# R of the lists built for 32 tokens at once, v tiles loaded behind the tokens, and a new timetable for splits, fills and checks in a Fourier-mixing plus expert-lookup kernel

## The chip, the cores and the metric

One core of one Trainium2 chip. The metric is the device time in microseconds of one execution. The kernel before has a median of 1169.77 us over 3 runs (1169.46 to 1169.96).

## The reference

```python
def _A_ref(x, dft_seq_re, dft_seq_im, dft_hid_re, dft_hid_im):   # x: 2048 x 512
    a = jnp.einsum("bsd,ed->bse", x, dft_hid_re)
    b = jnp.einsum("bsd,ed->bse", x, dft_hid_im)
    return jnp.einsum("ts,bse->bte", dft_seq_re, a) - jnp.einsum("ts,bse->bte", dft_seq_im, b)

def _B_ref(x, w_q, k1, k2, u, v):          # 32 heads, 64 + 64 keys of 128, 4096 experts of 512
    q = jnp.einsum("nd,dhc->nhc", xf, w_q)
    s1 = jnp.einsum("nhd,ed->nhe", q[..., :dk], k1)
    s2 = jnp.einsum("nhd,ed->nhe", q[..., dk:], k2)
    # the two largest of s1 and of s2, their four sums, the two largest of these: top_s, top_e
    g = _softmax(top_s, axis=-1)
    act = _gelu(jnp.einsum("nd,nhkd->nhk", xf, u[top_e]))
    return jnp.einsum("nhk,nhk,nhkd->nd", g, act, v[top_e])

xn = _layernorm(x, axis=-1)
return x + _A_ref(xn, ...) + _B_ref(xn, ...)
```

## The kernel before, in words

**Start (0 to about 85 us).** The tokens are normalised, the Fourier part runs as matmuls on folded matrices, and the tokens are transposed and split into two float16 parts (`xq`, also stored to `xt_d`).

**Score part (about 85 to 459 us).** Eight stages `j` of four heads, each with 16 blocks `i` of 128 tokens; 16j + i is the number by which tables place work. For a block PE does 12 matmuls (`scores`, L801) into one of four PSUM banks; ACT evicts the bank into a score tile `ss` (L806, four buffers); DVE takes the largest values and their indices (L809, L813). Beside that run, placed by tables of block numbers (`todo`, `at_k`, `slots`):

- `m_prep`: the raw weights `wq` of the next stage are split into two float16 parts, `wh` on ACT (L162), then a scaling of the raw tile on ACT (L167) or POOL (L169), then a subtraction on POOL (L170). Four tiles t a stage; PE multiplies them with the keys at L148 in blocks 3, 4, 5 and 7.
- `fill_uv`: the expert tables u and v are loaded, scaled twice on ACT (L613, L614) and split on POOL (L615) into resident tiles. `fill_far` does the same for v tiles 11 to 15, in blocks 104, 105, 106, 110 and 111, and stores them to DRAM (`v_d`), since their place in SBUF is taken until the score part ends.
- checks of the symmetries of the Fourier matrices (`compare`): two loads, a difference on POOL (L758, L764), and on the next block two absolute sums on ACT (L784 over 896 columns, L785 over 128). `EARLY` names the 32 that are done here; 36 others are done in the expert part.
- `routing` of the stage before, in blocks 1, 2 and 4: three sums on POOL (L651 to L653), comparisons on DVE (L654 onward), an exp on ACT (L659), casts into `z`.

Before a long ACT instruction of a fill, split or scale, `behind` copies the scale (128x1, L570) into spare columns of that block's score tile, and the instruction reads its scale from there.

**Passage.** The routing tile `z` goes to DRAM (`z_d`, L907); the first two blocks' lists are turned and widened (`cmp`, L704 and L705).

**Expert part (459 us to the end).** 15 blocks of 128 tokens (the 16th is done by gathers, one token's row at a time, on the side). For a block PE multiplies tokens `xb` with all u tiles (`u_part`, L959), ACT applies gelu (L962), and the gates come from `g_mm`: per half of 32 tokens (16) DVE compares the lists with counters into L (16 x 128 columns, L985) and R (16 x 32 columns, L990, then times the gate, L993), and PE multiplies L by R (L995). Products (L1005, L1012, L1015) feed `v_part` (L1024) over v tiles 0 to 15. Three pairs of L and R rotate. The other checks, and sums over weights (`fit`), run beside it in even steps.

Each engine works its queue in order; a planner fixes the order from the program's order and from hints that set order alone (`follow`, `hold`). SP issues nearly all loads and stores in order.

Of the kernel before, what the change touches and what calls it, by code (L numbers as in the profile page):

```python
# [36 lines left out]
def tile_fnet_peer(ctx, tc, x, ca, cb, c5, wt, wf, wr, wq, kt, ut, vn, uv, out):  # L37
# [55 lines left out]
    EARLY = [*range(8, 24), *range(40, 56)]  # L93
    early = cst.tile([P, 2, len(EARLY)], F32, name="early")
# [19 lines left out]
    k_sb = cst.tile([P, 2, 64], F32, name="k_sb")  # L114
    nc.sync.dma_start(k_sb, kt)
# [24 lines left out]
    def m_mul(j, t, kds):  # L140
        for kd in kds:
            if t == 0:
                MS.setdefault((j, "p"), []).append((pc if kd < 2 else pb)(f"m{j}_{kd}"))
            for hh in range(2):
                c0 = (t * 2 + hh) * 64
                if (j, t, "h") in MS:
                    for n, (l, r) in enumerate(((0, 0), (0, 1), (1, 0))):
                        nc.tensor.matmul(MS[j, "p"][kd][:, c0:c0 + 64],  # L148
                                         MS[j, t, "l" if l else "h"][:, hh, kd * P:(kd + 1) * P],
                                         k16[:, r, t // 2, :], start=n == 0, stop=n == 2)  # L150
                    continue
                nc.tensor.matmul(MS[j, "p"][kd][:, c0:c0 + 64], MS[j, t][:, hh, kd * P:(kd + 1) * P],
                                 k_sb[:, t // 2, :], start=True, stop=True)

    def m_prep(j, t, pool, at):

        raw = MS[j, t].rearrange("p h k -> p (h k)")
        MS[j, t, "h"] = pool.tile([P, 2, D], F16, tag="wh", name=f"wh{j}_{t}", bufs=4)
        h = MS[j, t, "h"].rearrange("p h k -> p (h k)")
        l = raw.bitcast(F16)[:, 0:2 * D]  # L160
        MS[j, t, "l"] = l.rearrange("p (h k) -> p h k", h=2)
        nc.scalar.activation(h, raw, AF.Copy, scale=at)  # L162
        if j == 1 and t % 2:
            nc.vector.scalar_tensor_tensor(l, raw, sw, h, op0=ALU.mult, op1=ALU.subtract)
            return
        if j == 1 or t > 1:
            nc.scalar.activation(raw, raw, AF.Copy, scale=at)  # L167
        else:
            nc.gpsimd.tensor_scalar(raw, raw, sw, None, op0=ALU.mult)  # L169
        nc.gpsimd.tensor_tensor(l, raw, h, op=ALU.subtract)  # L170
# [20 lines left out]
    def m_scale(j, pm, at=None):  # L191
# [10 lines left out]
        if w == 3:  # L202
            nc.scalar.activation(m[:, 0, 0:2].rearrange("p k n -> p (k n)"),
                                 MS[j, 3].rearrange("p h k -> p (h k)"), AF.Abs, accum_out=mx[:, KD + 1:KD + 2])
            nc.scalar.activation(m[:, 0, 0, 0:P], k_sb.rearrange("p w k -> p (w k)"), AF.Abs,
                                 accum_out=mx[:, KD + 2:])
# [27 lines left out]
    xtp = stS.enter_context(tc.tile_pool(name="xtp", bufs=1, side="left"))  # L234
    xq = [xtp.tile([P, 4, 2, KD, P], F16, name=f"xq{g}") for g in range(4)]
# [259 lines left out]
    nc.scalar.activation(k16[:, 0], k_sb, AF.Copy, scale=sk)  # L495
    nc.vector.scalar_tensor_tensor(k16[:, 1], k_sb, sk, k16[:, 0], op0=ALU.mult, op1=ALU.subtract)
# [58 lines left out]
    def part_b(safe, stS, stP, stE, xt, u_sb, cmp_p):  # L555
# [10 lines left out]
        def behind(src, at):  # L566

            if at is None:
                return src
            nc.scalar.activation(at, src, AF.Copy)  # L570
            return at


# [6 lines left out]
        def absmax(which, g, at):  # L580
            nc.scalar.activation(uf[15], uf[15], AF.Abs, scale=behind(one, at), accum_out=asums[:, g, which:which + 1])
# [22 lines left out]
        def fill_uv(which, g, at=None, dst=None):  # L604
            if dst is None:
                dst = (u_sb if which == 0 else v_sb)[g]
            s = behind(su if which == 0 else sv, at)
# [16 lines left out]
        def fill_far(g, at):  # L624
            t = wq_tile(f"vs{g}").rearrange("p h k -> p (h k)").bitcast(F16)
# [87 lines left out]
        def hold(f, after):  # L713
# [3 lines left out]
            for i in made[first:]:  # L717
                if i.engine in (mybir.EngineType.DVE, mybir.EngineType.Activation, mybir.EngineType.Pool):
# [7 lines left out]
        def compare(n, at=None):  # L726
# [54 lines left out]
            def judge():  # L781
                k = n if at is None else at
                a, b = (chk, asum) if at is None else (early[:, 0], early[:, 1])
                nc.scalar.activation(tf[:, P:], tf[:, P:], AF.Abs, accum_out=a[:, k:k + 1])  # L784
                nc.scalar.activation(tf[:, :P], tf[:, :P], AF.Abs, accum_out=b[:, k:k + 1])  # L785
# [9 lines left out]
        def scores(j, i, vals, idx):  # L795
# [8 lines left out]
            st = sp.tile([P, 520], F32, tag="s", name=f"ss{j}_{i}", bufs=3 if safe else 4)  # L804
            s = st[:, 0:512].rearrange("p (g e) -> p g e", g=2 * HC)
            nc.scalar.activation(s.rearrange("p g e -> p (g e)"), ps, AF.Copy, scale=inv)  # L806
# [9 lines left out]
            return st[:, 512:], mm  # L816
# [13 lines left out]
        else:  # L830
# [18 lines left out]
        for g, n in zip(range(V2, 16), () if safe else (104, 105, 106, 110, 111)):  # L849
# [8 lines left out]
        at_k = [13, 15] + [16 * j + i for j in range(1, 6) for i in (7, 8, 9, 10)]  # L858
        at_k += [101, 103, 108, 112, 118, 120, 122, 124, 125, 126]
# [7 lines left out]
        for j in range(NCH):  # L867
# [8 lines left out]
            for i in range(NT):  # L876
# [25 lines left out]
                for n, f in enumerate(todo[j * NT + i]):  # L902
                    f(spare[:, n:n + 1])
# [11 lines left out]
        LR = [(lr.tile([P, 16, P], F16, name=f"L{k}"), lr.tile([P, 16, NC], F16, name=f"R{k}")) for k in range(3)]  # L915
# [14 lines left out]
        for g in range(V2, 16 if not safe else V2):  # L930
            nc.sync.dma_start(v_sb[g].rearrange("p l c d -> p (l c d)"), v_d[g - V2])
# [7 lines left out]
        def prep(b):  # L939
            xb, act = BT[b] if b < 2 else blk_tiles(b)  # L940
            if b:
                nc.sync.dma_start(xb.rearrange("p a k n -> p (a k n)"), xt_d[b])
# [31 lines left out]
        def g_mm(b, tg, after=None):  # L974
            cmp = CMP[b]
            p = pg(f"g{b}_{tg}")
            for hf in range(2):
                ts = slice(tg * TG + hf * 16, tg * TG + hf * 16 + 16)

                def bc(w, n):  # L980
                    return cmp[:, w, ts, :].unsqueeze(2).to_broadcast([P, 16, n // 2, 2])

                LR.append(LR.pop(0))
                L, R = LR[-1]
# [3 lines left out]
                    bc(0, P), op=ALU.is_equal)  # L988
                Rv = R.rearrange("p t (c two) -> p t c two", two=2)
                nc.vector.tensor_tensor(  # L990
                    Rv, io_c.rearrange("p (c two) -> p c two", two=2).unsqueeze(1).to_broadcast([P, 16, NC // 2, 2]),
                    bc(1, NC), op=ALU.is_equal)
                nc.vector.tensor_tensor(Rv, Rv, bc(2, NC), op=ALU.mult)  # L993
                for t in range(16):
                    i = nc.tensor.matmul(p[:, hf, t * NC:(t + 1) * NC], L[:, t, :], R[:, t, :], start=True, stop=True)  # L995
# [226 lines left out]
        if not safe:  # L1222
            nc.vector.memset(chk[:, 68:70], 0.0)
            for k in range(0, len(EARLY), 16):
                for w, c in enumerate((chk, asum)):
                    nc.vector.tensor_copy(c[:, EARLY[k]:EARLY[k] + 16], early[:, w, k:k + 16])
        prep(0)
        prep(1)
        stP.close()
# [87 lines left out]
    with tc.If(r2 > 0):  # L1317
# [8 lines left out]
        xtp = stS.enter_context(tc.tile_pool(name="xtp2", bufs=1, side="left"))  # L1326
        xt = [xtp.tile([P, 2, KD, P], F16, name=f"xs{i}") for i in range(NT)]
# [127 lines left out]
```

## Time and profile before

| | |
|---|---|
| median of 3 runs | 1169.77 us |
| the profiled execution | 1169.36 us |
| its span in the trace | 1167.5 us |
| mean granted TensorE clock | 0.986 |
| score part, first to last block on PE | about 72 to 459 us |
| expert part, one block on PE | 45.5 us |

Rows of the stretches read: from:to, length, then busy us and instructions (x) of PE, weight loads, DVE, ACT and POOL, then the granted clock, the DMA share and GB/s. Rows of the waits read: who <- whom: us in total, times, longest. Timeline rows read: start, length, engine, line, operation, count, and in brackets the idle time before it with what ended it. Group rows read: count | busy us, mean ns | idle before, with what ended it.

### The profile page before, as it was taken

Reading aid. Unit: us, or ns where it says so; the run is one execution under the profiler, and the core shown is the slowest. Engines: PE = TensorE matmul, PEld = TensorE weight load, DVE = VectorE, ACT = ScalarE, POOL = GpSimd, SP = SyncE. Lnnn points to the kernel's source line nnn. Section 1 sums busy time; section 2 is a strip of 40 time slices with the busy share of each in tenths; the row PEclk is TensorE's granted clock in tenths of the full one; section 3 lists DMA queues with packets and bytes.
Section 4 is the critical chain, followed back from the end, with each engine's and each line's share of the span. In section 5 each row is a group of like instructions: output and inputs, shape, how many; then the busy total and the mean of one; then the engine's idle time right before and its main releaser. Section 6 shows DMA issues by size and latency. Waiting matters only on the chain.

```text
span 1167.5 us, 29293 instructions
## 1 busy us (share of the span) xinstructions
PE 1115.2 (96%) x11681; PEld 732.7 (63%) x11681; DVE 906.0 (78%) x2790; ACT 670.3 (57%) x1257; POOL 480.0 (41%) x442
## 2 busy tenths in 40 slices
PE   5799999999999988699999999999999999999997
PEld 4354555454444434696786786876876867868763
DVE  7878888797977978767888777677878876777861
ACT  3575666877867877332654654654646455556450
POOL 0021848678778777100413433334233243233320
PEclk9899999999999999899999999999999999999999
DMA  8255254442533463622445535443554355355401
GB/s 311 78 214 202 84 188 163 127 161 76 180 130 106 152 201 97 216 69 73 119 132 164 166 98 171 148 140 112 163 168 130 115 163 164 116 153 157 110 11 48
DMA packets 75074, 162.79 MB, mean 139 GB/s; under 512 B 9254, under 2 KB 26157, under 8 KB 74928
## 3 DMA queue, kind: packets, MB, share of 16 engines
q1 hardware_dynamic: 63250, 123.07, 31.8%
q0 software_dynamic: 11520, 37.75, 11.8%
q8 instruction: 93, 1.52, 0.5%
q14 instruction: 53, 0.43, 0.1%
q10 hardware_dynamic: 158, 0.01, 0.0%
HBM read 143.96 MB, written 16.84 MB: 138 GB/s over the span
## 4 chain that ended last, share of the span: by engine, by line
PE 74%; POOL 11%; DVE 6%; issue 4%; DMA 2%; ACT 1%; SPq 0%; POOLq 0%; DVEq 0%; ACTq 0%
PE v L1024 27%; PE z L959 26%; PE s L801 13%; PE g L995 4%; POOL cx L758 2%; POOL v L615 2%; PE p L370 2%; POOL u L615 2%; POOL wq L169 1%; POOL wq L170 1%; PE m L148 1%; POOL vs L615 1%; DVE vals L809 1%; DMA xb<-xt_d 1%; DVE idx L813 1%
## 5 line engine op out<-in xcount | busy, mean ns | idle before, releaser
L801 PE MATMUL s<-m,xq 128*128 128x512 f16 x1536 | 341.7, 380 | 10.1 <-ACT ss L806 10.0
L959 PE MATMUL z<-xb,u 128*128 128x128 f16 x5760 | 333.4, 220 | 12.3 <-DMA xb<-xt_d 8.4
L959 PEld LDWEIGHTS <-u 128*128 128x128 f16 x5760 | 326.8, 98 | 16.0 <-issue 13.0
L1024 PE MATMUL v<-v,act 128*128 128x512 f16 x1440 | 319.9, 379 | 0.0
L801 PEld LDWEIGHTS <-xq 128*128 128x128 f16 x1536 | 148.8, 98 | 184.1 <-issue 14.8
L1084 POOL TENSOR_TENSOR ov<-ov,ga 128x512 f32<-128x512 f32 x64 | 95.0, 1484 | 396.7 <-ACT ga L1079 319.7
L1024 PEld LDWEIGHTS <-act 128*128 128x128 f16 x1440 | 137.5, 98 | 156.7
L985 DVE TENSOR_TENSOR L<-io_lam,cmp 128x2048 f16<-128x2048 f16 x120 | 150.3, 1253 | 102.3 <-PE g L995 71.4
L962 ACT ACTIVATE act<-z,scl 128x512 f32<-128x512 f32 x120 | 81.6, 682 | 192.0 <-PE z L959 188.3
L809 DVE MAX8 vals<-ss 128x8 f32<-128x64 f32 x1024 | 152.9, 216 | 21.9 <-ACT ss L806 21.8
L1050 POOL DMA_INDIRECT ga<-in_uv_dram,eix x64 | 93.4, 1460 | 52.1 <-PE z L959 24.5
L1015 DVE TENSOR_TENSOR act<-w,act 128x1024 f16<-128x1024 f32 x60 | 80.1, 1336 | 41.5 <-ACT act L1012 38.4
L813 DVE FIND_INDEX8 idx<-vals,ss 128x8 uint16<-128x256 f32 x256 | 107.2, 419 | 0.0
L1012 ACT ACTIVATE act<-w 128x1024 f16<-128x1024 f32 x60 | 80.8, 1346 | 21.1 <-DVE w L1005 21.0
L806 ACT ACTIVATE ss<-s,wsc 128x512 f32<-128x512 f32 x112 | 74.3, 675 | 24.2 <-PE s L801 22.3
L784 ACT ACTIVATE cx<-cx 128x896 f32<-128x896 f32 x64 | 60.6, 947 | 31.2 <-POOL cx L764 11.3
L1005 DVE SCALAR_TENSOR_TENSOR w<-act,scl,g 128x1024 f32<-128x1024 f32 x60 | 76.0, 1273 | 1.4 <-ACT fit L1152 1.1
L758 POOL TENSOR_TENSOR cx<-cx 128x512 f32<-128x512 f32 (+2 forms) x56 | 61.7, 1120 | 20.4 <-DMA cx<-in_cb_dram 18.2
L170 POOL TENSOR_TENSOR wq<-wq,wh 128x1024 f16<-128x1024 f32 x26 | 55.4, 2132 | 19.7 <-DMA wq<-in_wq_dram 16.1
L995 PEld LDWEIGHTS <-L 128*128 128x128 f16 x1920 | 55.8, 96 | 8.5 <-issue 1.8
L995 PE MATMUL g<-R,L 128*128 128x32 f16 x1920 | 57.5, 176 | 1.4 <-DVE R L993 1.4
L993 DVE TENSOR_TENSOR R<-R,cmp 128x512 f16<-128x512 f16 x120 | 57.1, 476 | 2.0
(276 smaller groups left out, 1255.7 us busy)
## 6 DMA issues: line engine op xcount, KB each, us to landing
cx<-in_cb_dram SPq DMA_DIRECT2D x64, 448.0 KB
wq<-in_wq_dram SPq DMA_DIRECT2D x32, 512.0 KB
fit<-in_wq_dram SPq DMA_DIRECT2D x28, 512.0 KB
uv<-in_ut_dram SPq DMA_DIRECT2D x16, 512.0 KB
uv<-in_vn_dram SPq DMA_DIRECT2D x16, 512.0 KB
xq<-in_x_dram SPq DMA_DIRECT2D x8, 512.0 KB
xt_d<-xq SPq DMA_DIRECT2D x16, 256.0 KB
cx<-in_ca_dram SPq DMA_DIRECT2D x64, 64.0 KB
```

Of the source, the lines that this page charges most:

```text
L758: v_eng.tensor_tensor(v, v, tv[:, 0:1].to_broadcast([P, len(ix), 256]), op=o)
L801: mm = nc.tensor.matmul(ps, xt[i][:, l, kd, :], m[:, r, kd, :], start=(n == 0), stop=(n == 3 * KD - 1))
L809: nc.vector.max(vals[:, i, w, :, h], s[:, g, :])
L813: nc.vector.max_index(idx[:, i, w].rearrange("p k h -> p (k h)"), vals[:, i, w, 0:2].rearrange("p k h -> p (k h)"), s[:, w * HC:g + 1, :]. ...
L959: mm = nc.tensor.matmul(p[:, cc * P:(cc + 1) * P], ug[:, l, c % 2, kd, :], xb[:, r, kd, :], start=(n == 0), stop=(n == 3 * KD - 1))
L962: GL[mm.ins.name] = nc.scalar.activation(act[:, cg * 4:cg * 4 + 4, :].rearrange("p c n -> p (c n)"), p, AF.Gelu_apprx_tanh, scale=zsc)
L985: nc.vector.tensor_tensor(L.rearrange("p t (l two) -> p t l two", two=2), io_lam.rearrange("p (l two) -> p l two", two=2).unsqueeze(1).to_ ...
L995: i = nc.tensor.matmul(p[:, hf, t * NC:(t + 1) * NC], L[:, t, :], R[:, t, :], start=True, stop=True)
L1012: i = nc.scalar.activation(w16[..., 0], w, AF.Copy)
L1024: mm = nc.tensor.matmul(pv, w16[:, c, :, l], vg[:, r, c % 2, :], start=(c == 0 and k == 0), stop=(c == NC - 1 and k == 2))
L1050: nc.gpsimd.indirect_dma_start(out=t, out_offset=None, in_=uv, in_offset=bass.IndirectOffsetOnAxis(ap=eix[:, n].rearrange("p k h -> p (k h ...
L1084: T["a"] = nc.gpsimd.tensor_tensor(o, o, t, op=ALU.add)
```

## The change

- `g_mm`: R is built once for 32 tokens (32 x 32 columns) with its first half and used by both; two R buffers in place of three; L stays at 16 tokens and three buffers.
- The loads of v tiles 11 to 15 stand behind the load of block 1's tokens (`xb`) in SP's queue.
- `behind` and its copies go. The ACT work of a block is kept behind that block's eviction by an order hint (`hold` with ACT alone).
- `m_prep`: of the later stages, only tile 0 is scaled on POOL; tile 1 is scaled on ACT as 2 and 3 are. The four tiles come one block earlier (11, 13, 15 of the stage before, and 1).
- Fills of stages 3 to 6 move from blocks 4, 6, 11, 13 to 3, 5, 12, 14; the far fills from 104 to 111 to block 10 of stages 2 to 6, through a buffer of the checks (`cx`).
- 28 checks in place of 32 in the score part, in blocks 0, 4, 6 and 7 of most stages; four move to the expert part. An early check sums 896 columns only; its other sum is set to zero.
- The key tile `k_sb` moves to the pool of the tokens; the score tile loses its 8 spare columns.

```diff
-    EARLY = [*range(8, 24), *range(40, 56)]
-    early = cst.tile([P, 2, len(EARLY)], F32, name="early")
+    EARLY = [*range(8, 24), *range(40, 52)]
+    early = cst.tile([P, len(EARLY)], F32, name="early")
...
-        if j == 1 or t > 1:
+        if j == 1 or t:
             nc.scalar.activation(raw, raw, AF.Copy, scale=at)
         else:
             nc.gpsimd.tensor_scalar(raw, raw, sw, None, op0=ALU.mult)
...
-        def behind(src, at):
-            if at is None:
-                return src
-            nc.scalar.activation(at, src, AF.Copy)
-            return at
...
         def fill_far(g, at):
-            t = wq_tile(f"vs{g}").rearrange("p h k -> p (h k)").bitcast(F16)
+            t = sp.tile([P, 4, 4, 64], F32, tag="cx", name=f"vs{g}", bufs=3)
+            t = t.rearrange("p s q c -> p (s q c)").bitcast(F16)
...
             def judge():
                 k = n if at is None else at
-                a, b = (chk, asum) if at is None else (early[:, 0], early[:, 1])
+                a = chk if at is None else early
                 nc.scalar.activation(tf[:, P:], tf[:, P:], AF.Abs, accum_out=a[:, k:k + 1])
-                nc.scalar.activation(tf[:, :P], tf[:, :P], AF.Abs, accum_out=b[:, k:k + 1])
+                if at is None:
+                    nc.scalar.activation(tf[:, :P], tf[:, :P], AF.Abs, accum_out=asum[:, k:k + 1])
...
-                    todo[1 + t if j == 1 else (j - 1) * NT + 2 * t - 4].append(
-                        lambda at, j=j, t=t: m_prep(j, t, wqp, behind(sw, at)))
+                    todo[1 + t if j == 1 else (j - 1) * NT + 2 * t - 5].append(
+                        lambda at, j=j, t=t: m_prep(j, t, wqp, sw))
...
-        slots = [29, 31, 36, 43, 45] + [16 * j + i for j in range(3, 7) for i in (4, 6, 11, 13)]
+        slots = [29, 31, 36, 43, 45] + [16 * j + i for j in range(3, 7) for i in (3, 5, 12, 14)]
...
-        for g, n in zip(range(V2, 16), () if safe else (104, 105, 106, 110, 111)):
+        for g, n in zip(range(V2, 16), () if safe else [16 * j + 10 for j in range(2, 7)]):
...
-        at_k = [13, 15] + [16 * j + i for j in range(1, 6) for i in (7, 8, 9, 10)]
-        at_k += [101, 103, 108, 112, 118, 120, 122, 124, 125, 126]
+        at_k = [10, *(16 + i for i in (0, 4, 6, 7, 10)), *(16 * j + i for j in range(2, 7) for i in (0, 4, 6, 7)), 112, 125]
...
-                for n, f in enumerate(todo[j * NT + i]):
-                    f(spare[:, n:n + 1])
+                for f in todo[j * NT + i]:
...
+                        hold(lambda: f(None), spare, (mybir.EngineType.Activation,))
...
-        for g in range(V2, 16 if not safe else V2):
-            nc.sync.dma_start(v_sb[g].rearrange("p l c d -> p (l c d)"), v_d[g - V2])
...
         prep(0)
         prep(1)
+        for g in range(V2, 16 if not safe else V2):
+            i = nc.sync.dma_start(v_sb[g].rearrange("p l c d -> p (l c d)"), v_d[g - V2])
+            follow(i.ins, T["xb"])
...
             for hf in range(2):
-                LR.append(LR.pop(0))
-                L, R = LR[-1]
+                LS.append(LS.pop(0))
+                L = LS[-1]
...
+                if hf == 0:
+                    RS.append(RS.pop(0))
+                    R = RS[-1]
+                    Rv = R.rearrange("p t (c two) -> p t c two", two=2)
+                    nc.vector.tensor_tensor(
+                        Rv, io_c.rearrange("p (c two) -> p c two", two=2).unsqueeze(1)
+                        .to_broadcast([P, TG, NC // 2, 2]), bc(1, 0, TG, NC), op=ALU.is_equal)
+                    nc.vector.tensor_tensor(Rv, Rv, bc(2, 0, TG, NC), op=ALU.mult)
```

SP's queue at the passage, before: `z_d` is the store of the routing, `v_d` the far v tiles, `xb` the tokens of block 1, `oy` and `zb` loads for later blocks.

```order
L907 DMA z_d<-z 128x12x384
L931 DMA v_5929<-v_d 128x2048
L931 DMA v_5930<-v_d 128x2048
L931 DMA v_5931<-v_d 128x2048
L931 DMA v_5932<-v_d 128x2048
L931 DMA v_5933<-v_d 128x2048
L942 DMA xb_5940<-xt_d 128x1024
```

The same place in SP's queue after the change:

```order
L905 DMA z_d<-z 128x12x384
L939 DMA xb_5812<-xt_d 128x1024
L1230 DMA v_5806<-v_d 128x2048
L1230 DMA v_5807<-v_d 128x2048
L1230 DMA v_5808<-v_d 128x2048
L1230 DMA v_5809<-v_d 128x2048
L1230 DMA v_5810<-v_d 128x2048
```

The tokens' load has moved from behind the five v tiles to ahead of them. Next, ACT's queue at the boundary from stage 4 to stage 5, before: `ss` are evictions (from `s`) and, from `wsc`, the small copies; `wh` and `wq` are splits, `m` a sum over weights, `c` the exp of the routing.

```order
L806 ACTIVATE ss_15_3961<-s_15_3948,wsc 128x512
L570 ACTIVATE ss_0_3988<-wsc 128x1
L189 ACTIVATE m_4382,sums<-m_3744 128x2048
L162 ACTIVATE wh_2_4001<-wq_2_3792,ss_0_3988 128x1024
L806 ACTIVATE ss_0_3988<-s_0_3975,wsc 128x512
L167 ACTIVATE wq_2_3792<-wq_2_3792,ss_0_3988 128x1024
L659 ACTIVATE c_0_4032<-c_0_4030 128x64
L806 ACTIVATE ss_1_4018<-s_1_4005,wsc 128x512
```

The same boundary in ACT's queue after the change (`cx` is the sum of a check):

```order
L801 ACTIVATE ss_15_3930<-s_15_3917,wsc 128x512
L161 ACTIVATE wh_2_3942<-wq_2_3762,wsc 128x1024
L188 ACTIVATE m_4354,sums<-m_3723 128x2048
L166 ACTIVATE wq_2_3762<-wq_2_3762,wsc 128x1024
L801 ACTIVATE ss_0_3961<-s_0_3948,wsc 128x512
L778 ACTIVATE cx_3882,early<-cx_3882 128x896
L801 ACTIVATE ss_1_3991<-s_1_3978,wsc 128x512
L161 ACTIVATE wh_3_4018<-wq_3_3764,wsc 128x1024
L653 ACTIVATE c_0_4009<-c_0_4007 128x64
```

The exp has moved behind the eviction of block 1, a check has come to stand between the evictions of blocks 0 and 1, and the small copies are gone. Last, DVE's queue for a group of 32 tokens in the expert part, before:

```order
L985 TENSOR_TENSOR L_5914<-io_lam,cmp_14719 128x2048
L990 TENSOR_TENSOR R_5915<-io_c,cmp_14719 128x512
L985 TENSOR_TENSOR L_5916<-io_lam,cmp_14719 128x2048
L993 TENSOR_TENSOR R_5915<-R_5915,cmp_14719 128x512
L990 TENSOR_TENSOR R_5917<-io_c,cmp_14719 128x512
L993 TENSOR_TENSOR R_5917<-R_5917,cmp_14719 128x512
```

DVE's queue for such a group after the change:

```order
L980 TENSOR_TENSOR L_5794<-io_lam,cmp_15274 128x2048
L980 TENSOR_TENSOR L_5792<-io_lam,cmp_15274 128x2048
L988 TENSOR_TENSOR R_5795<-io_c,cmp_15274 128x1024
L991 TENSOR_TENSOR R_5795<-R_5795,cmp_15274 128x1024
L1014 TENSOR_TENSOR act_14522<-w_3_15631,act_14522 128x32x32
```

Two R instructions of twice the length stand where four stood, and both L stand ahead of them.

More of the change, by code (lines that the diff above doesn't have):

```diff
@@ L113, in tile_fnet_peer @@
     zsc, fw, osc = scl[:, 0:1], scl[:, 1:2], scl[:, 2:3]
-    k_sb = cst.tile([P, 2, 64], F32, name="k_sb")
-    nc.sync.dma_start(k_sb, kt)
+    K = []
     usc = cst.tile([P, 6], F32, name="usc")
@@ L580, in absmax @@
         def absmax(which, g, at):
-            nc.scalar.activation(uf[15], uf[15], AF.Abs, scale=behind(one, at), accum_out=asums[:, g, which:which + 1])
+            nc.scalar.activation(uf[15], uf[15], AF.Abs, scale=one, accum_out=asums[:, g, which:which + 1])
         def uv_scale():
@@ L606, in fill_uv @@
                 dst = (u_sb if which == 0 else v_sb)[g]
-            s = behind(su if which == 0 else sv, at)
+            s = su if which == 0 else sv
             raw = RAW.pop((which, g))
@@ L717, in hold @@
             for i in made[first:]:
-                if i.engine in (mybir.EngineType.DVE, mybir.EngineType.Activation, mybir.EngineType.Pool):
+                if i.engine in engines:
                     follow(i, after)
```

49 lines of the change are left out of this document (27 added, 22 removed).

## The prediction

> **What bounds the kernel now.** I read the page's engine shares and chain first, then busy time by stretches, then PE's waits, then the timelines of PE, SP, ACT and DVE where PE waits.
>
> ```profile
> PE 1115.2 (96%) x11681; PEld 732.7 (63%) x11681; DVE 906.0 (78%) x2790; ACT 670.3 (57%) x1257; POOL 480.0 (41%) x442
> PE 74%; POOL 11%; DVE 6%; issue 4%; DMA 2%; ACT 1%; SPq 0%; POOLq 0%; DVEq 0%; ACTq 0%
> ```
>
> PE is busy for 96% of the span, yet the chain runs over PE for only 74%. The stretches show where the difference lies.
>
> ```profile
> 270.00:290.00 20.00, 20.00 (x157) 10.19 (x156) 13.54 (x68) 13.45 (x20) 17.44 (x23) 1.00 0.18 55
> 410.00:430.00 20.00, 16.36 (x73) 7.03 (x72) 13.12 (x81) 17.05 (x31) 12.83 (x17) 1.00 0.72 235
> 545.00:590.00 45.00, 45.00 (x608) 33.79 (x606) 36.82 (x67) 24.72 (x47) 12.37 (x9) 1.00 0.53 152
> 1000.00:1045.00 45.00, 45.00 (x610) 33.96 (x609) 33.51 (x53) 24.34 (x48) 13.65 (x11) 1.00 0.48 144
> ```
>
> The first pair after the length is PE. From 545 us on PE never stops, so nothing that makes another engine quicker there can show. PE has holes late in the score part (to 459 us) and in the passage to the expert part (459 to 505 us). Its waits between 85 and 520 us:
>
> ```profile
> PE s L801 <- ACT ss L806: 10.0, 8, 3.4
> PE z L959 <- DMA xb<-xt_d: 8.4, 1, 8.4
> PE m L148 <- POOL wq L170: 2.8, 3, 1.3
> PE g L995 <- DVE R L993: 1.4, 1, 1.4
> PE z L959 <- ACT cmp L705: 1.3, 1, 1.3
> ```
>
> 12.8 us are lost in the score part (an eviction late on ACT, a split late on POOL) and 11.1 us in the passage. Two waits cost more than their length:
>
> ```profile
> 385.72 15.70 PE L801 MATMUL s<-m,xq 128*128 128x512 f16 x72
> 441.89 17.39 PE L801 MATMUL s<-m,xq 128*128 128x512 f16 x72 [3.42 <-ACT ss L806]
> 494.97 5.28 PE L959 MATMUL z<-xb,u 128*128 128x128 f16 x48 [8.40 <-DMA xb<-xt_d]
> 500.90 5.52 PE L959 MATMUL z<-xb,u 128*128 128x128 f16 x96
> 480.00:495.00 15.00, 6.04 (x121) 5.59 (x119) 8.45 (x12) 2.97 (x4) 3.86 (x3) 0.83 0.91 339
> ```
>
> After the wait of 3.42 us the same 72 matmuls take 1.7 us longer; after that of 8.40 us 48 take what 96 take later, about 2.6 us more, and the stretch around it has a granted clock of 0.83. All that PE could win is 12.8 + 1.7 + 11.1 + 2.6 = 28.2 us.
>
> [...]
>
> **The tokens ahead of the v tiles.** The SP queue shows the one large wait:
>
> ```profile
> 473.32 0.38 SPq L907 DMA_DIRECT2D z_d<-z  x1
> 479.62 2.38 SPq L931 DMA_DIRECT2D v<-v_d  x5
> 482.05 0.50 SPq L942 DMA_DIRECT2D xb<-xt_d  x1
> 521.66 2.53 PE L1024 MATMUL v<-v,act 128*128 128x512 f16 x11
> 1143.17 0.34 SPq L1032 DMA_DIRECT2D y<-y_d  x1
> 1146.73 1.06 POOL L1033 DMA_DIRECT2D y<-in_x_dram  x1 [5.20 <-DMA y<-y_d]
> ```
>
> SP stands until the store of the routing has landed, asks for five v tiles of 512 KB, and only then for block 1's tokens (256 KB), which arrive at 494.97. Now the tokens go first, at 479.6. A transfer of their size with the queue to itself took 3.6 us (1143.17 to 1146.73), so they are there at 483.2, before PE is through block 0's z at 486.6: the 8.4 us and the 2.6 us go. The v tiles follow 0.5 us later and were needed only some 50 us on (tile 11 starts 66 of 96 matmuls into block 0's v part, which begins at 521.7). The two loads that stand behind them (oy, zb) move by the same 0.5 us and gate nothing before 530 us.
>
> **The score part.** A stage of 16 row blocks costs PE 44.2 us: 16 x 2.59 (31.08/12, below) + 4 x 0.70.
>
> ```profile
> 204.10 31.08 PE s L801 x144
> 153.16 0.70 PE m L148 x24
> L170 POOL TENSOR_TENSOR wq<-wq,wh 128x1024 f16<-128x1024 f32 x26 | 55.4, 2132 | 19.7 <-DMA wq<-in_wq_dram 16.1 <-ACT wq L167 2.6
> L169 POOL TENSOR_SCALAR wq<-wq,wsc 128x1024 f32<-128x1024 f32 x12 | 34.2, 2847 | 14.6 <-ACT wh L162 14.6
> L167 ACT ACTIVATE wq<-wq,ss 128x1024 f32<-128x1024 f32 x14 | 16.1, 1148 | 0.2
> L785 ACT ACTIVATE cx<-cx 128x128 f32<-128x128 f32 x32 | 9.6, 301 | 0.0
> L570 ACT ACTIVATE ss<-usc 128x1 f32<-128x1 f32 x32 | 6.1, 197 | 15.0 <-DVE idx L813 15.0
> ACT c L659 <- POOL c L656: 22.1, 5, 5.1
> ACT cx L784 <- POOL cx L764: 11.3, 12, 2.3
> 327.56 0.26 ACT L659 ACTIVATE c<-c 128x64 f32<-128x64 f32 x1 [5.12 <-POOL c L656]
> ```
>
> At a stage boundary POOL worked off two scalings and two splits (10 us) before it came to the routing; ACT stood 5.1 us at the exp, with the evictions of blocks 1 and later queued behind it, until PE had no free bank. Six stages lose one scaling on POOL (6 x 2.85 = 17 us) and get one on ACT (6 x 1.15 = 7 us). ACT loses 60 small copies (the 32 shown and 28 of the other two scales; 60 x 0.2 = 12 us, and the 15.0 us that they waited for a score tile) and 28 sums of 128 columns with their read-outs (28 x 0.5 = 14 us). The five far fills, until now all in blocks 104 to 111, come one to a stage. Stage 7 keeps two checks of seven, one of them in its last five blocks where three had stood.
>
> What stays: ACT still meets checks between two evictions, and each waits for POOL. I laid out one loaded stage (3 to 5) by these durations: at its start POOL waits for DVE to finish the last block (some 3 us in), does the three routing sums and the check, and ACT passes that check about 7 us in and the exp at once. Eviction 8 then falls 32.8 us in, where PE needs it at 33.9. From stage to stage ACT and POOL together are 1.1 to 1.7 us slower than PE, so PE waits 0 in stage 3, 0.7 in 4, 1.6 in 5 and some 1.2 in 6, which has no splits at its end: 3.5 us of estimate, between 0 and the 12.8 of now. I take 3.5, since the 5.1 us wait that caused most is gone. Gain 12.8 + 1.7 - 3.5 = 11.0.
>
> **The passage.** With no check behind blocks 13 to 15, the eviction of the last block and the copy of cmp follow at once, so the 1.3 us goes. The 1.4 us was the second half's R; now R is ready with the first half. A remainder of 1.0 us I leave for DVE:
>
> ```profile
> 459.11 0.50 PE L704 MATMUL zt<-ident,z 128*128 128x128 f16 x6
> 467.97 0.42 DVE L813 FIND_INDEX8 idx<-vals,ss 128x8 uint16<-128x256 f32 x1
> ```
>
> DVE ended its last block 9.3 us after PE had ended the scores (468.4 against 459.1); without the checks ahead of ACT's last evictions I take 7. From there the tokens need 15.8 us: 4.9 to the store as now (473.3), 0.5 for the longer R in between, 6.3 until it has landed, 0.5 and 3.6 for the tokens. PE asks for them 24.8 us after its last score (486.6 - 459.1, less waits of 2.7). The slack is 2.0 us, which a late DVE can eat. Gain 11.1 + 2.6 - 1.0 = 12.7.
>
> **The expert part.**
>
> ```profile
> L985 DVE TENSOR_TENSOR L<-io_lam,cmp 128x2048 f16<-128x2048 f16 x120 | 150.3, 1253 | 102.3 <-PE g L995 71.4
> L993 DVE TENSOR_TENSOR R<-R,cmp 128x512 f16<-128x512 f16 x120 | 57.1, 476 | 2.0
> L990 DVE TENSOR_TENSOR R<-io_c,cmp x120: 398/418/1497, 470.1 to 1125.9; 128x512 f16<-128x512 f16 x120
> ```
>
> R of twice the length should take 0.73 us, between 0.476 and 1.253 by length; 120 of them in place of 240 save DVE some 26 us. Four more checks cost DVE and ACT about 2 us each. PE covers both: priced at 0, for better or worse, while DVE waits 71 us for PE to free an L. If that cover went, a group of 32 tokens would be ready 1.8 us later than now, since both L now stand ahead of R (2 x 1.25 + 2 x 0.73 against 1.25 + 2 x 0.48).
>
> The k tile in another pool, and the early sums set to zero, touch nothing that is waited for.
>
> **Sum.** The profiled execution took 1169.36 us (span 1167.5), 0.4 below the median of 1169.77. 1169.4 - 11.0 - 12.7 = 1145.7, so 1146 us. Its own range is 1141 (everything won) to 1150 (4 us more left).
>
> **Rivals.** *The evictions stay late.* ACT gets more long work per stage (a fill and a scaling more) and waits at the checks in order, so the 10.0 us and the 1.7 us of restart remain: 1157.4 at worst, 1154 with a third of it won. For it: ACT waited 11.3 us at checks already. Chance 0.13.
>
> *DVE holds the passage.* If DVE ends its last block when it does now, PE merely reaches block 1's z earlier and waits for the tokens, at 483.2 in place of 494.97; the score gain is lost there: 1169.4 - 11.8 = 1157.6. For it: DVE was 19.4 of 20 us busy from 430 to 450. Against: it waited 24.8 us for POOL and 21.8 us for ACT in the score part, which shrink.
>
> ```profile
> 430.00:450.00 20.00, 16.04 (x66) 6.87 (x66) 19.37 (x105) 13.83 (x23) 15.58 (x17) 0.91 0.39 121
> DVE pm L654 <- POOL c L653: 24.8, 7, 4.8
> DVE vals L809 <- ACT ss L806: 21.8, 22, 3.3
> ```
>
> Chance 0.09. It is also the case in which the change does not do what it says, because tokens and v tiles wait for the same store.
>
> *Slower: DVE late in the expert part.* If PE waits for L and R, 60 times, 0.40 us each eats the gain. Should the 21 groups for which DVE had not been ahead (60 less the 39 halves with a wait) show the full 1.8 us, that is 37 us: 1183. Against it: PE waited once for R in all. [...] Chance 0.07.
>
> **How the numbers follow.** The forecast has 0.68, the rivals 0.13, 0.09 and 0.07, nothing at all 0.03. Faster takes the first three, 0.90; same 0.03; slower 0.07. A change of 0.2% is what a measurement of this kernel can tell. The range, 1141 to 1158, holds the forecast and both lesser gains.
>
> **What would show it.** PE's wait for xb gone and the stretch 480 to 495 at full clock; PE's waits for ss under 5 us in all and the splits' wait gone; the exp's wait under 1 us; blocks of the expert part still 45.5 us apart. I am wrong if PE waits for xb again, if ss waits stay near 10 us, or if g waits for R or L after 545 us.

## The result, and the profile after

The changed kernel takes 1157.37 us (median of 4 runs, 1155.13 to 1158.98) against 1169.62 us before: a ratio of 0.9897, 95% interval 0.9878 to 0.9916. Faster by 12 us, where 23.7 were forecast. The profiled execution took 1157.38 us (span 1155.5), 11.98 less than the one of before, so the two traces can be set side by side, stage by stage.

PE's waits of the changed kernel between 85 and 520 us (us in total, times, longest):

```profile
PE s L796 <- ACT ss L801: 10.4, 7, 2.3
PE m L147 <- DVE u L457: 3.9, 1, 3.9
PE g L993 <- DVE L L980: 0.5, 1, 0.5
```

The waits for xb, cmp and R are gone, as forecast, and so is the wait for the splits. The one for late evictions, forecast at 3.5, is 10.4, and a wait of 3.9 us for a DVE result stands where there was none.

PE's timeline gives the stage ends. First the changed kernel, from its first score to its last run of products:

```profile
71.92 1.24 PE L796 MATMUL s<-m,xq 128*128 128x512 f16 x5
...
463.16 0.50 PE L698 MATMUL zt<-ident,z 128*128 128x128 f16 x6
...
534.60 8.20 PE L956 MATMUL z<-xb,u 128*128 128x128 f16 x144
...
1099.63 2.84 PE L956 MATMUL z<-xb,u 128*128 128x128 f16 x48 [1.64 <-ACT act L959]
...
1117.75 31.24 PE L1023 MATMUL v<-v,act 128*128 128x512 f16 x144
```

The same places of the kernel before:

```profile
71.95 1.24 PE L801 MATMUL s<-m,xq 128*128 128x512 f16 x5
...
544.70 8.20 PE L959 MATMUL z<-xb,u 128*128 128x128 f16 x144
...
1110.13 4.30 PE L959 MATMUL z<-xb,u 128*128 128x128 f16 x48 [2.03 <-ACT act L962]
...
1129.74 31.24 PE L1024 MATMUL v<-v,act 128*128 128x512 f16 x144
```

Both start their scores at 71.9 us. The scores end at 463.16 against 459.11: the score part is 4.05 us **longer**. From there to block 2 of the expert part it is 71.44 us against 85.59: the passage is 14.15 us shorter. From block 2 to the last run of products it is 583.15 against 585.04, 1.9 us shorter. 4.05 - 14.15 - 1.9 = -12.0.

So the passage paid for everything, and the half of the change that moves splits, fills and checks brought less than nothing. In the score part PE lost 10.4 + 3.9 us in waits and two restarts at low clock:

```profile
195.03 0.26 PE L147 MATMUL m<-sums,wh 128*128 128x64 f16 x2 [3.87 <-DVE u L457]
195.32 5.30 PE L796 MATMUL s<-m,xq 128*128 128x512 f16 x12
201.15 2.75 PE L796 MATMUL s<-m,xq 128*128 128x512 f16 x12
315.25 20.88 PE L796 MATMUL s<-m,xq 128*128 128x512 f16 x96 [1.07 <-ACT ss L801]
359.62 25.16 PE L796 MATMUL s<-m,xq 128*128 128x512 f16 x108 [2.28 <-ACT ss L801]
```

12 matmuls took 5.30 us in place of 2.75 (2.55 lost, granted clock 0.51); 108 took 25.16 where 23.49 is due by the rate of the 96 (1.67 lost, granted clock 0.68 in the first 5.4 us). Together 10.4 + 3.9 + 2.55 + 1.67 = 18.5 us, against 10.0 + 2.8 + 1.7 = 14.5 before: the 4 us.

**Where the evictions become late.** Between 85 and 520 us ACT waits 49.3 us for POOL at the checks (L778 for L758), where it waited 11.3 us before. In each of stages 3 to 6 it stands 6.2 to 8.6 us at the check of block 4 and 2.9 to 3.4 us at that of block 6. ACT's timeline in a loaded stage (stage 5, counted from 0), the changed kernel. L801 is an eviction, L606 and L607 are the two halves of a fill, L778 is a check:

```profile
343.25 0.67 ACT L801 ACTIVATE ss<-s,wsc 128x512 f32<-128x512 f32 x1
350.12 0.95 ACT L778 ACTIVATE cx<-cx 128x896 f32<-128x896 f32 x1 [6.21 <-POOL cx L758]
...
351.07 0.67 ACT L801 ACTIVATE ss<-s,wsc 128x512 f32<-128x512 f32 x1
351.64 1.13 ACT L606 ACTIVATE u<-uv,usc 128x1024 f16<-128x1024 f32 x1
352.81 1.15 ACT L607 ACTIVATE uv<-uv,usc 128x1024 f32<-128x1024 f32 x1
353.86 0.67 ACT L801 ACTIVATE ss<-s,wsc 128x512 f32<-128x512 f32 x1
357.95 0.95 ACT L778 ACTIVATE cx<-cx 128x896 f32<-128x896 f32 x1 [3.42 <-POOL cx L758]
...
358.90 0.67 ACT L801 ACTIVATE ss<-s,wsc 128x512 f32<-128x512 f32 x1
```

And POOL at the same time (L169 a split, L656 the gates, L608 a fill's subtraction, L752 and L758 a check's differences):

```profile
339.24 2.13 POOL L169 TENSOR_TENSOR wq<-wq,wh 128x1024 f16<-128x1024 f32 x1
...
341.81 2.13 POOL L169 TENSOR_TENSOR wq<-wq,wh 128x1024 f16<-128x1024 f32 x1
344.93 0.32 POOL L656 TENSOR_TENSOR g<-c,g 128x64 f32<-128x64 f32 x1 [0.98 <-DVE g L655]
...
345.46 2.13 POOL L608 TENSOR_TENSOR u<-uv,u 128x1024 f16<-128x1024 f32 x1
347.54 2.01 POOL L752 TENSOR_TENSOR cx<-cx 128x512 f32<-128x512 f32 x2
349.63 0.46 POOL L758 TENSOR_TENSOR cx<-cx 128x128 f32<-128x128 f32 x1
...
354.03 2.13 POOL L608 TENSOR_TENSOR u<-uv,u 128x1024 f16<-128x1024 f32 x1 [3.26 <-ACT uv L607]
```

At block 4 ACT comes to the check with its evictions done and stands 6.21 us. POOL, which had two splits in front of that check, has just ended the second of them (343.94); still to come are a wait of 0.98 us for DVE, the gates, the subtraction of block 3's fill (2.13 us) and the check's own differences (2.5 us). Behind the check stand evictions 5 to 7 and the fill of block 5. Now the roles turn: POOL has run ahead of that fill and stands 3.26 us until ACT has done it (353.96), and ACT then stands 3.42 us at the check of block 6, which on POOL comes after that subtraction. Eviction 7 starts at 358.90, and PE, out of free banks, starts again at 359.62 after 2.28 us. Each of the two engines waits for the other, one after the other.

### The profile page after: what moved, and what is told of

It reads as the page before. It is cut to its first block, busy times and chain, and to the rows that moved or that the text cites. A ratio compares the mean times of both kernels' runs of the same rounds, so it can differ in the third digit from the quotient of the medians.

```text
span 1155.5 us, 29027 instructions
## 1 busy us (share of the span) xinstructions
PE 1115.2 (97%) x11681; PEld 729.8 (63%) x11681; DVE 916.0 (79%) x2682; ACT 658.3 (57%) x1145; POOL 446.5 (39%) x424
## 4 chain that ended last, share of the span: by engine, by line
PE 66%; DVE 14%; POOL 10%; issue 6%; ACT 3%; DMA 1%; POOLq 0%; DVEq 0%; ACTq 0%
PE v L1023 26%; PE z L956 24%; PE s L796 7%; PE g L993 4%; DVE vals L804 2%; POOL u L608 2%; DVE idx L808 2%; POOL wq L169 2%; POOL cx L752 2%; PE p L371 2%; DMA v_d<-vs 1%; DVE L L980 1%; POOL vs L608 1%; POOL cx L758 1%; POOL v L608 1%
## 5 line engine op out<-in xcount | busy, mean ns | idle before, releaser
L796 PE MATMUL s<-m,xq 128*128 128x512 f16 x1536 | 344.7, 382 | 10.5 <-ACT ss L801 10.4
L956 PE MATMUL z<-xb,u 128*128 128x128 f16 x5760 | 329.0, 219 | 1.7 <-ACT act L959 1.6
L956 PEld LDWEIGHTS <-u 128*128 128x128 f16 x5760 | 323.0, 98 | 5.0 <-issue 2.0
L1049 POOL DMA_INDIRECT ga<-in_uv_dram,eix x64 | 89.6, 1400 | 38.5 <-POOL ov L1083 19.1
L778 ACT ACTIVATE cx<-cx 128x896 f32<-128x896 f32 x64 | 60.5, 946 | 76.6 <-POOL cx L758 49.3
L801 ACT ACTIVATE ss<-s,wsc 128x512 f32<-128x512 f32 x112 | 73.9, 679 | 30.4 <-PE s L796 23.9
L169 POOL TENSOR_TENSOR wq<-wq,wh 128x1024 f16<-128x1024 f32 x26 | 55.4, 2131 | 24.8 <-DMA wq<-in_wq_dram 15.9
L752 POOL TENSOR_TENSOR cx<-cx 128x512 f32<-128x512 f32 (+2 forms) x48 | 54.0, 1139 | 13.8 <-PE hy L445 7.1
L699 ACT ACTIVATE cmp<-zt 128x768 f16<-128x768 f16 x15 | 12.0, 810 | 72.5 <-PE zt L698 72.5
```

The lines of the kernel that those rows point to most:

```text
L796: mm = nc.tensor.matmul(ps, xt[i][:, l, kd, :], m[:, r, kd, :], start=(n == 0), stop=(n == 3 * KD - 1))
L956: mm = nc.tensor.matmul(p[:, cc * P:(cc + 1) * P], ug[:, l, c % 2, kd, :], xb[:, r, kd, :], start=(n == 0), stop=(n == 3 * KD - 1))
L1049: nc.gpsimd.indirect_dma_start(out=t, out_offset=None, in_=uv, in_offset=bass.IndirectOffsetOnAxis(ap=eix[:, n].rearrange("p k h -> p (k h ...
```

## The experiments

Each kernel changes one thing against the kernel that is named (e6 puts back the whole timetable); its rows carry its own line numbers, which may differ by one. "Score part" is the time from the first score to the first zt row on PE (387.2 us before, 391.2 in the changed kernel), "rest" from there to the last run of products (670.6 and 654.6).

**e1, the v tiles alone.** The kernel before, with the five loads moved:

```diff
-        for g in range(V2, 16 if not safe else V2):
-            nc.sync.dma_start(v_sb[g]..., v_d[g - V2])
...
         prep(1)
+        for g in range(V2, 16 if not safe else V2):
+            i = nc.sync.dma_start(v_sb[g]..., v_d[g - V2])
+            follow(i.ins, T["xb"])
```

> The kernel before with one edit: the five v tiles are asked for behind the rows xb of blocks 0 and 1. Theory (the passage's gain is this order of transfers and nothing else): the 8.4 us wait for xb and the 2.6 us of slow clock behind it go, the waits for cmp (1.3) and R (1.4) stay, the score part is as before: 1169.4 - 11.0 = 1158 us. Rival (the passage could only become short because the last checks were taken out of its way): DVE still ends its last block 9 us after PE, PE waits for block 1's tokens instead, and no more than 5 us is won: 1164 or above.

1157.15 us (1154.56 to 1158.91), ratio 0.9912 [0.9886, 0.9937]. PE's waits between 85 and 520 us:

```profile
PE s L801 <- ACT ss L806: 10.0, 8, 3.5
PE m L148 <- POOL wq L170: 2.7, 3, 1.3
PE z L957 <- ACT cmp L705: 1.5, 1, 1.5
PE g L993 <- DVE R L991: 1.4, 1, 1.4
```

The 8.4 us for xb are gone and all the others are as before to within 0.2 us. The rest is 657.5 us, 13.1 shorter (of that 1.5 are a slow restart in the tail that this execution lacks: 48 matmuls took 4.30 us before and 2.84 here). The rival falls: the checks did not have to leave the passage first. This one edit is as fast as the whole change, as far as the two intervals tell.

**e2, the checks back.** The changed kernel, with

```diff
-        at_k = [10, *(16 + i for i in (0, 4, 6, 7, 10)), *(16 * j + i for j in range(2, 7) for i in (0, 4, 6, 7)), 112, 125]
+        at_k = [13, 15] + [16 * j + i for j in range(1, 6) for i in (7, 8, 9, 10)]
+        at_k += [101, 108, 112, 118, 122, 125]
```

> The changed kernel with the 28 checks put back to the blocks of before (13, 15, then blocks 7 to 10 of stages 1 to 5, then 101, 108, 112, 118, 122, 125). Theory (the checks at blocks 4, 6 and 7 hold ACT, because POOL reaches them only after two splits, the gates and a fill's subtraction): the 6.2 us waits of ACT at the check of block 4 go, PE's waits for ss fall from 10.4 to under 5 us, the score part ends 5 to 8 us earlier, 1150 to 1152 us. Rival 1 (what the stages carry in all is too much, above all the far fills): waits stay near 10 us, 1156 to 1159. Rival 2 (the splits one block earlier cost stage 2 its 3.9 us wait and slow clock): that wait stays here as it is.

1138.57 us (1138.30 to 1140.35), ratio 0.9753 [0.9728, 0.9777]: 11 us under the 1150 to 1152 that were expected. Between 85 and 520 us PE waits only in the passage, 0.2 us for cmp and:

```profile
PE g L994 <- DVE L L981: 1.8, 1, 1.8
```

The score part is 370.9 us, 20.3 shorter than in the changed kernel; 18.5 of that are the waits and slow restarts counted above. Rival 1 (the stages carry too much) falls: stages 2 to 5, far fills and all, carry the same work with no wait. (Two checks have gone from stage 6 to 7 and one from stage 1 to 0; e10 and e7 below leave them in their stages.) Rival 2 falls in its form: the 3.9 us of stage 2 went although the splits stayed early.

**e10, one check of each stage.** The changed kernel with the check of block 4 at block 9:

```diff
-... i in (0, 4, 6, 7, 10)), ... i in (0, 4, 6, 7)), 112, 125]
+... i in (0, 6, 7, 9, 10)), ... i in (0, 6, 7, 9)), 112, 125]
```

> The changed kernel with only the check of block 4 moved to block 9, in stages 1 to 6; fills at 3, 5, 12 and 14 and checks at 0, 6 and 7 stay. Theory (ACT stands 6.2 us at the check of block 4, behind which the evictions of blocks 5 to 7 queue): PE's waits for ss fall from 10.4 to under 2 us, stage 2 keeps its 3.9 us and slow clock: 1143 to 1146. Rival (POOL and ACT are loaded, and the wait only moves on to the check of block 6): 5 us or more of ss waits stay, 1150 or above.

1146.08 us (1144.45 to 1146.92), 0.9810 [0.9782, 0.9838].

```profile
PE m L147 <- DVE u L457: 3.9, 1, 3.9
...
PE s L796 <- ACT ss L801: 0.4, 1, 0.4
```

For PE the wait did not move on to block 6: 10.4 us became 0.4. ACT still stands at the check of block 6 (3.34 us in stage 5), and that alone does not reach PE. With the fills at 3 and 5 it is enough to take away the check of block 4; stage 2 kept its 3.9 us.

**e3, the fills back instead.** The changed kernel with `(3, 5, 12, 14)` again `(4, 6, 11, 13)`, checks untouched.

> The changed kernel with the fills of stages 3 to 6 at blocks 4, 6, 11 and 13 again, the checks left at 0, 4, 6 and 7. Theory (POOL reaches the check of block 4 late because of two splits, the gates and the subtraction of block 3's fill): without that subtraction ahead of it ACT waits some 2 us less at block 4 (4 in place of 6.2), more at block 6; PE's waits for ss fall from 10.4 to between 4 and 9 us, 1151 to 1156. If the fills next to the checks are the whole cause, it comes near e2: 1140 to 1145.

1143.36 us (1140.87 to 1144.38), 0.9784 [0.9759, 0.9810]; no wait for an eviction at all in the score part. That is more than the theory gave it, and in the range of the other case. ACT's timeline in the same stage shows why:

```profile
334.39 1.14 ACT L606 ACTIVATE u<-uv,usc 128x1024 f16<-128x1024 f32 x1
...
341.12 0.95 ACT L778 ACTIVATE cx<-cx 128x896 f32<-128x896 f32 x1 [4.41 <-POOL cx L758]
...
342.07 1.25 ACT L801 ACTIVATE ss<-s,wsc 128x512 f32<-128x512 f32 x2
343.21 1.14 ACT L606 ACTIVATE u<-uv,usc 128x1024 f16<-128x1024 f32 x1
```

And POOL's:

```profile
338.57 1.99 POOL L752 TENSOR_TENSOR cx<-cx 128x512 f32<-128x512 f32 x2
...
341.05 2.14 POOL L608 TENSOR_TENSOR u<-uv,u 128x1024 f16<-128x1024 f32 x1
```

ACT still waits 4.41 us at block 4's check. But two evictions follow it at once, no fill and no second check stand between them, and POOL finds the next fill done: the check's differences now stand ahead of the fill's subtraction, and not behind it. At the two checks that follow in this stage, ACT waits 0.16 us at most. So neither the fills nor the checks are too many, nor is either place bad by itself. A stand of ACT of 3.3 us at block 6 alone (e10) or of 4.4 us at block 4 alone (e3) did not reach PE; the two of the changed kernel, one behind the other with a fill between them, did. Whether the 6.2 us alone would have been too much was not tried.

**e7, the check of block 0 kept.** The changed kernel with the checks of blocks 4, 6 and 7 at 8, 9 and 10:

```diff
-... i in (0, 4, 6, 7, 10)), ... i in (0, 4, 6, 7)), 112, 125]
+... i in (0, 7, 8, 9, 10)), ... i in (0, 8, 9, 10)), 112, 125]
```

> The changed kernel with the three checks of blocks 4, 6 and 7 moved to blocks 8, 9 and 10, the check at block 0 kept, in stages 1 to 6 (stage 1 has five: 0, 7, 8, 9, 10). If the checks of blocks 4 to 7 are the cause, ACT no longer waits 6.2 us there and the score part ends within 3 us of e2: 1139 to 1143. If the check at block 0 is a cause too (2 us of POOL between the routing's first operations, in stage 2 ahead of what DVE and PE wait for), stage 2 keeps its 3.9 us wait and its 2.5 us of slow clock: 1145 to 1148.

1142.39 us (1141.14 to 1143.19), 0.9774 [0.9753, 0.9795]. In stages 3 to 7 PE waits for nothing, and stage 2 kept its 3.9 us and its slow clock (0.77 from 190 to 205 us); the score part, 377.8 us, is 6.9 longer than e2's. So by the traces both cases of the expectation hold: the checks of blocks 4 to 7 cost stages 3 to 6, that of block 0 costs stage 2. The total is 2.6 us under the 1145 to 1148 given for that; 1.8 of it is that the rest came out shorter than e2's (654.4 against 656.3).

**e9, fills back and block 32's check moved.** e3 with

```diff
-... for j in range(2, 7) for i in (0, 4, 6, 7)), 112, 125]
+... for j in range(2, 7) for i in (9 if j == 2 else 0, 4, 6, 7)), 112, 125]
+        at_k.sort()
```

> e3 (the changed kernel with the fills at blocks 4, 6, 11 and 13) with one check more moved: that of block 32, the first of stage 2, to block 41. If that check is what DVE and PE wait for in stage 2 (2 us of POOL between the routing's first sums and the numbers that DVE needs for u), the 3.9 us wait and the 2.5 us of slow clock go and nothing else changes: 6.4 us under e3, 1136 to 1138. Rival (the split that now comes one block earlier stands there as well and is enough by itself): the wait stays at 2 us or more, 1140 to 1143.

1137.38 us (1136.84 to 1137.70), 0.9738 [0.9712, 0.9765], the lowest median of all, level with e2 by the intervals. PE's waits between 85 and 520 us come to one line:

```profile
PE m L147 <- POOL wq L169: 0.2, 1, 0.2
```

What stood there in the changed kernel, POOL's rows of stage 2 and the DVE operation that waits for them:

```profile
181.97 1.96 POOL L752 TENSOR_TENSOR cx<-cx 128x512 f32<-128x512 f32 x2
186.98 2.13 POOL L169 TENSOR_TENSOR wq<-wq,wh 128x1024 f16<-128x1024 f32 x1
189.07 0.32 POOL L677 TENSOR_TENSOR i2s<-if,i2s 128x64 f32<-128x64 f32 x1
189.43 2.14 DVE L681 SCALAR_TENSOR_TENSOR di<-c,i2s 128x64 int32<-128x64 f32 x1 [2.60 <-POOL i2s L677]
```

The check's differences (L752) stand between the routing's operations on POOL, and the split stands ahead of the last one that DVE needs (L677). DVE waited 2.60 us, and u, the last thing that DVE does for PE here, ended at 194.9. In e9 the order is L677 at 186.26, then the split: with the check away the split too has gone behind L677. The rival falls: the split one block earlier makes no wait by itself. The score parts of e3 and e9 differ by 4.65 us, which are the 3.9 us and 0.6 less for a split; the 2.5 us of slow clock that the 6.4 counted did not occur in e3's trace (granted clock 1.00 from 190 to 205 us).

**e4, the far fills back** at blocks 104 to 111: `[16 * j + 10 for j in range(2, 7)]` again `(104, 105, 106, 110, 111)`.

> The changed kernel with the five far fills put back to blocks 104 to 111 (their tile as in the changed kernel). Theory (order of checks and fills): stages 3 to 6 keep PE's waits of about 2 us at blocks 1 and 8, since no far fill stands between the splits and the check of block 4; 1155 to 1158, or worse, as stage 6 gets all five. Rival 1 (the far fills overload the stages): each stage loses 2.3 us of ACT and 2.1 us of POOL, the waits of stages 3 to 5 go, score part shorter by 5 us or more, 1152 or less unless stage 6 loses it again.

1166.34 us (1163.86 to 1167.81), 0.9978 [0.9965, 0.9991]; PE's waits:

```profile
PE s L796 <- ACT ss L801: 17.9, 12, 4.8
```

Of these 11.4 us fall after 398 us. In stages 3 to 5, freed of them, PE waited 6.5 us where the changed kernel waits 7.5. Rival 1 falls again; spreading the far fills is worth 9 us in the changed kernel.

**e5, the splits one block later again**: `2 * t - 5` back to `2 * t - 4`.

> The changed kernel with the four splits of a stage one block later again, as before (scaling of the second still on ACT). Rival 2 (the earlier split stands ahead of the routing on POOL in stage 2, DVE waits 2.6 us for it and PE 3.9 us for u, and then runs 12 matmuls at half clock): that wait and the 2.5 us of slow clock go, 6.4 us won in stage 2. Theory adds that in stages 3 to 6 the last split comes at block 2 in place of 1 and pushes the check of block 4 later by about 2 us, so that PE waits 2 us more in each of four stages: 1157.4 - 6.4 + 0 to 8 = 1151 to 1159, the stage 2 wait gone in any case.

1155.79 us (1155.10 to 1156.99), 0.9897 [0.9872, 0.9922], the same as the changed kernel. The stage 2 wait shrank to 1.8 us and did not go, and the waits for evictions grew to 12.3: inside the range, but the statement that the wait goes in any case was wrong. With the split behind L677 and the check still there, 1.8 us are left: the split is one cause there, the check of block 32 the other.

**e6, the whole timetable back.** Checks as in e2, fills as in e3, far fills as in e4, splits as in e5 and the second scaling on POOL (`if j == 1 or t > 1`).

> The changed kernel with the whole timetable of the score part put back: checks at the blocks of before (28 of them), fills at blocks 4, 6, 11 and 13, far fills at blocks 104 to 111, the splits one block later and the second scaling on POOL again. It differs from e2 by the other half of the timetable. If that half (splits, scaling, fills, far fills) is worth what was forecast, some 11 us, PE's waits of about 10 us for ss and 2.7 us for the splits come back: 1150 to 1157. If the checks' number and the missing copies did it alone, it is as fast as e2, 1139 to 1142.

1153.84 us (1151.97 to 1156.21), 0.9882 [0.9858, 0.9907].

```profile
PE s L796 <- ACT ss L801: 9.9, 6, 2.9
```

The wait for the splits did not come back, that for evictions did, and with it ACT's wait for POOL at the exp of the routing:

```profile
ACT c L653 <- POOL c L650: 33.4, 6, 6.6
```

In e2 that wait is 3.7 us, once. Two of the six waits of PE, 2.15 and 2.89 us, end within 2 us of such a stand of ACT; the other four were not traced. The score part is 383.7 us against 370.9 in e2, which has the same checks: the other half of the timetable (far fills spread, splits earlier, one scaling on ACT, fills at 3 and 5) is worth 12.8 us in these two traces when the checks do not undo it; by the medians it is 15.

**e8, R for 16 tokens again**, in e2.

> e2 with R made for 16 tokens at a time again, as before. The prediction priced R for 32 tokens at nothing: same time as e2 within 1.5 us (1137 to 1141), blocks of the expert part 45.5 us apart in both. What could differ: PE waited 1.8 us for L in e2's passage, and waits 1.4 us for R here. If the longer R carried part of the gain, this is slower by 2 us or more.

1141.39 us (1140.87 to 1142.39), 0.9771 [0.9750, 0.9792] against e2's 0.9753 [0.9728, 0.9777]; the medians are 2.8 us apart, more than the 1.5 that was expected, but the intervals overlap, so that the times alone decide nothing. The trace shows a difference, in PE's waits and its timeline:

```profile
PE g L992 <- DVE R L990: 3.3, 2, 3.0
```

```profile
460.14 6.90 PE L956 MATMUL z<-xb,u 128*128 128x128 f16 x96
```

In the passage PE waits 3.0 us for the second half's R, where e2 waits 1.8 for L, and the next 96 matmuls take 6.90 us, which take 5.52 in e2: 2.6 us together. From 520 us on PE waits in both only once, at the end (1.0 and 1.7 us). So R for 32 tokens helped a little in these two traces, at the one place where DVE is behind, and nowhere else.

## Why the prediction was right in its sign and where it was wrong

- **The passage: right.** Forecast 12.7 us, measured 14.15. The waits for xb, R and cmp went; 0.5 us for L remained where 1.0 was left for DVE, and the other 0.95 us were not traced. The mechanism was tested alone by e1, which came out at 1157 where 1158 was expected. DVE's rival did not come: its last block ended 8 us after PE's scores (471.3 against 463.2) where 7 was assumed, and the slack held. One reason given does not stand: a check is still placed at block 125, which is block 13 of the last stage, and e6, with the checks of e2, waits 1.3 us for cmp where e2 waits 0.2. What else that wait hangs on stays open.
- **The score part: wrong, and this is the step that failed.** The prediction laid out one loaded stage by durations and found eviction 8 in time, with a residue of 3.5 us; PE lost 18.5. The layout names the check of the stage's start and the exp; of the other checks the prediction says that each waits for POOL, but it gives these waits no length. It did not carry POOL's list forward to the same place: two splits, the gates and a subtraction in front of block 4's check. They measured 6.2 us and more at block 4 and some 3 us at block 6; with the other checks it is 49.3 us. Work per stage was counted, and that was right: ACT and POOL can do it, as e9 shows, in which every stage keeps its checks and fills.
- **Its bound was wrong too.** The residue was given between 0 and the 12.8 us of now, that is, never worse than before; the waits alone came to 14.3. The new 3.9 us wait in stage 2 was not among the things considered; a check had been put between routing operations, and on POOL it was never placed against what DVE needs there.
- **The gain of 11 us was there.** With the checks at the blocks of before (e2) the score part is 16.2 us shorter than before. The other half of the timetable is 12.8 of that (e6 against e2); the remaining 3.4, e6 against before, go with fewer checks, fewer sums and no copies, which no run takes apart. The changed kernel lost 20.3 us again by where it put its checks. The mechanism that was forecast shows in the changed kernel: at the starts of stages 3 to 6, where ACT stood up to 5.1 us at the exp, it does not wait there any more. The 7.2 us that are left, where under 1 was forecast, are 0.9 early in the score part and 6.3 in stage 7, where PE waits for nothing.
- **The expert part: right.** No wait of PE for L or R after 545 us, and blocks 45.5 us apart (534.60 to 580.12). The 1.9 us gained there are 0.4 of a shorter wait in the tail and 1.5 of a restart at low clock that did not occur (48 matmuls in 4.30 us at a granted clock of 0.63 before, in 2.84 us at 1.00 now). These two are no part of what was forecast. The longer R takes 0.68 us, the median of 60, where 0.73 was given.

Of the rivals, "the evictions stay late" (chance 0.13) comes closest: PE's waits for evictions stayed near 10 us, which the prediction also names as a sign that it is wrong. Its reason was half right. ACT did wait at the checks in order, but the long work was not too much: e9, with the same work in every stage, has no late eviction. That its 1157.4 meets the measured 1157.37 is luck. The 1157.4 equals 1145.7 with the 10.0 and the 1.7 put on top, although 3.5 us of waits were in the 1145.7 already; with the splits' 2.8 us won and nothing else in the score part, the prediction's own terms give 1169.4 - 12.7 - 2.8 = 1153.9. The measured time is made of other terms: the score part 4.05 us longer, and the passage and the end 16.05 us shorter. It is luck as well that the time lies inside the range, which ends at 1158: without the 1.9 us at the end, which no term of the prediction holds, it would not.

## What to carry to other kernels

Where two in-order engines hand work to each other in both directions, count not only the work of each but the order of the hand-overs: write down both lists side by side, and ask at each wait what the other engine still has in front of the thing waited for. Here a fill goes from ACT to POOL and a check from POOL to ACT, and where the two alternated, each engine stood for the other in turn (in stage 5 ACT 6.21 us, POOL 3.26 us, ACT 3.42 us). Moving one check per stage (e10), or the fills by one block (e3), won more than 10 us with the same instructions.

And change the timetable apart from the rest: e1 alone gave all that the whole change gave, which hid that the score part had a gain of 16.2 us in it and a loss of 20.3.

## What the hardware showed that was not expected

**Whether PE restarted at low clock did not follow from the length of the wait.** Three stretches right behind a wait; the third figure from the end is the granted clock. The changed kernel, behind the 3.87 us:

```profile
195.30:198.00 2.70, 2.70 (x11) 1.02 (x9) 2.70 (x12) 0.00 (x0) 2.45 (x3) 0.50 0.83 241
```

e6, behind a wait of 2.15 us:

```profile
372.90:375.50 2.60, 2.55 (x7) 0.87 (x7) 2.60 (x9) 2.57 (x3) 1.98 (x2) 0.51 0.00 0
```

e3, behind a wait of 3.89 us:

```profile
196.50:199.20 2.70, 2.70 (x22) 1.29 (x19) 2.70 (x12) 0.00 (x0) 2.34 (x3) 1.00 0.65 219
```

Half clock after 3.87 us and after 2.15 us, full clock after 3.89 us at the same place of the program as the 3.87. e7's 12 matmuls there took 5.07 us after 3.89 us too. In e6 the 48 matmuls behind a wait of 2.89 us took 10.72 us, 0.2 more than 48 behind 1.29 us (10.52), where the 12 behind the shorter 2.15 us took 4.43, 1.7 more than 12 at 367.34 (2.75). What makes the slow restarts was not tried.

**A small DVE operation lasted as long as the one on POOL beside it.** L681 on 64 columns has a median of 0.225 us and once 2.14 us, at 189.43, when a subtraction on POOL ran from 189.35 to 191.48:

```profile
L681 DVE SCALAR_TENSOR_TENSOR di<-c,i2s x9: 167/225/2140, 139.7 to 474.3; 128x64 int32<-128x64 f32 x7, 128x16 int32<-128x16 f32 x1, 128x48 int32<-128x48 f32 x1
```

In e9 the same operation lasts 2.14 us again, from 186.61, beside a split on POOL that runs from 186.53 to 188.67, and its median of nine there is 2.13 us. So in the routing, where DVE and POOL pass small pieces to each other, L681 took some 1.9 us more than its median in the changed kernel beside a subtraction (L608), and again beside a split (L169), from which it takes nothing; what ties the two together no run shows. In e9 PE did not wait for it: its one wait between 85 and 520 us is 0.2 us, for a split.
